# Held loads and moved state tiles in a fused S5 and long-convolution kernel

## The chip, the cores and the metric

The kernel runs on one core of one Trainium2 chip, as one program. The metric is device time in microseconds (us) of one execution; lower is better. A profiled execution gives the trace from which the rows below are taken. The engines are named as the trace names them: PE is the matrix engine, PEld its weight loads, DVE the vector engine, ACT the scalar engine, POOL the engine that issues the accumulating DMAs, SP the engine that issues nearly all other DMAs.

## The reference, cut to what matters

Two sequence layers read the same input `x` of 2048 positions and 1024 channels, and a gate mixes them.

```python
g = sigmoid((x * gate_w).sum(-1, keepdims=True))

# a: a diagonal complex state-space layer (S5)
Lam_bar = exp(dt * Lam)
Bu = einsum("bld,pd->blp", x, ((Lam_bar - 1.0) / Lam)[:, None] * Bmat)
for t in range(L):
    h = Lam_bar[None, :] * h + Bu[:, t, :]
    hs.append(h)
a = 2.0 * einsum("blp,dp->bld", stack(hs), Cmat).real + x * Dskip

# b: a short convolution of k, times v, then a long convolution by FFT
kv = (4-tap causal convolution of k with shift_k) * v
y = irfft(rfft(kv, 4096) * rfft(ssm_k, 4096))[:2048]
b = x * (y + kv * ssm_D)

out = g * a + (1 - g) * b
```

All inputs and the output are bfloat16.

## The kernel before, in words

The kernel first computes the long convolution (the "convolution stage", up to about 222 us), and then the state layer, the gate and the mix (the "state stage").

The convolution works on 8 chunks of 128 channels. For a chunk `n`, PE does the taps of the short convolution (`taps`, from the transposed `kT`), mirrors and transforms the filter (`mirror_K` from `kn`, then `fwd_K`) and the product kv (`times_v`, then `fwd_V`) with cosine and sine tables; ACT copies each transform from PSUM (`Kh`, which is kept in a part of BT 3 for even chunks, and `Vh`). DVE multiplies the two spectra in blocks (`products`, into `G`, with the scratch `wkh` and BT 2). PE then transforms back (`inverse`), ACT copies the result to `cv`, and SP stores it to a scratch in DRAM (`cv_scr`).

Some additions are not done by DVE but by DMAs that accumulate in SBUF. `gather` (line 125) issues them from POOL's queue: `G += wkh` in `products` (768 KB per chunk), `ks += lo` in `times_v`, `eok += lo` in `mirror_K`, and `hr += hr` in `turn_table`. DVE waits for the first of them in the middle of `products` (`G[:, :, 2:] += n1`).

The loads go through SP's queue, which issues in order. Those named `kn`, `kT`, `BT` and `xT` are transposing DMAs of 512 KB each (`load_t`, line 119; `xT` is one such load for each half of a block of 512 positions); `v` is a plain copy of 1 MB for two chunks, and `cv_scr` are plain stores. `load` (line 172) makes `kn`, `kT` and `v` of a chunk, `load_BT` (line 211) one half of a group of the state layer's B, `load_xT` (line 214) the transposed x of a block.

The order of the work is written out by hand. Helpers (`mm`, `tt`, `act` and so on, over `put` at line 91) fix the order on each engine as the order in which the program issues. The generators (`products`, `times_v`, `mirror_K`, `inverse`, `Bu_tile`, `turn_table`) yield between steps, and the loop at line 901 steps through them. In its pass `c`, called chunk c here, DVE does the products of chunk c, PE the inverse of chunk c - 1, the transforms of chunk c + 1, and the taps and mirror of chunk c + 2, and SP issues the loads of chunk c + 3.

Into this loop tiles of the state layer's first matmul are woven (`Bu_tile`: 32 matmuls of 128x256 with BT and xT, two copies of U by ACT, and a few matmuls with `lamd`, which `lam_diag` prepares on DVE). There are 12 of them, from the generator at line 899. Line 955 places one ahead of `fwd_K` in chunks 3 to 6, line 975 one ahead of `fwd_V` in chunks 2 and 4 and two in chunk 6; four are left for the time behind the loop. Chunk 1 and chunk 0 have none. Four tiles each use xT 0, xT 1 and xT 2, in this order; those that use xT 2 are the four behind the loop.

Of the kernel before, what the change touches and what calls it, by code (L numbers as in the profile page):

```python
# [10 lines left out]
ACT = mybir.ActivationFunctionType  # L11
# [9 lines left out]
def kernel(  # L21
# [40 lines left out]
    HB = TB // 2  # L62
    NG = NP // 2
    NC = D // 128
# [3 lines left out]
    def pool(name, bufs, **kw):  # L68
        return ctx.enter_context(tc.tile_pool(name=name, bufs=bufs, **kw))
# [6 lines left out]
    lam_pool = pool("lam", 1)  # L76
# [8 lines left out]
    def ps2(shape, name):  # L85
        return psum.tile(shape, F32, name=name, tag="ps")
# [4 lines left out]
    def put(eng, f, *a, **kw):  # L91
        with tc.issue_after(prev[eng]) if eng in prev else nullcontext():
            i = f(*a, **kw)  # L93
        prev[eng] = getattr(i, "ins", i)

    def mm(o, l, r, first, last):
        put("pe", nc.tensor.matmul, o, lhsT=l, rhs=r, start=first, stop=last)
# [9 lines left out]
    def ts(o, a, s1, s2, op0, op1=None):  # L107
        if op1 is None:
            put("dve", V.tensor_scalar, out=o, in0=a, scalar1=s1, scalar2=None, op0=op0)
        else:  # L110
            put("dve", V.tensor_scalar, out=o, in0=a, scalar1=s1, scalar2=s2, op0=op0, op1=op1)
# [4 lines left out]
    def act(o, i, **kw):  # L116
        put("act", nc.scalar.activation, out=o, in_=i, **kw)

    def load_t(o, i):
        put("sp", nc.sync.dma_start_transpose, out=o, in_=i)  # L120

    def move(o, i):
        put("sp", nc.sync.dma_start, out=o, in_=i)
# [37 lines left out]
    pih = consts.tile([128, 1], F32, name="pih")  # L161
# [7 lines left out]

    lds = {}  # L170

    def load(which, c):
        cc = slice(c * 128, (c + 1) * 128)
        if which == "kn":

            t = ld.tile([128, NT, 128], BF16, name="kn", tag="ld")
            load_t(t, B_ssm_k[cc, :])
        elif which == "v":

            w = 1 if c < 2 else 2  # L180
            if w == 1:
                t = ld.tile([128, NT, 1, 128], BF16, name="v", tag="ld")
            else:
                t = xt_pool.tile([128, NT, 2, 128], BF16, name="v2", tag="xT")
            move(t.rearrange("p n k d -> p n (k d)"),
                 vf.rearrange("(n p) d -> p n d", p=128)[:, :, c * 128:(c + w) * 128])
            for k in range(w):
                lds["v", c + k] = t[:, :, k]
            return
        else:  # L190

            t = ld.tile([128, PAD + S], BF16, name="kT", tag="ld")
            put("pool", nc.gpsimd.memset, t[:, 0:PAD], 0.0)
            load_t(t[:, PAD:], kf[:, cc])
        lds[which, c] = t
# [13 lines left out]
    xTs = {}  # L209

    def load_BT(g, c):
        load_t(BT[g][:, c], (A_B_re, A_B_im)[c][g * 256:(g + 1) * 256, :])

    def load_xT(tb, halves=(0, 1)):
        if 0 in halves:
            xTs[tb] = (xt_pool if tb in (1, 2) else xt_first).tile([128, ND, TB], BF16, name="xT", tag="xT")
        for h in halves:
            load_t(xTs[tb][:, :, h * HB:(h + 1) * HB], xf[tb * TB + h:(tb + 1) * TB:2, :])


# [297 lines left out]
    def spectrum(which, c):  # L518
        if which == "K" and c % 2 == 0:

            t = BT[3].rearrange("p c d q -> p (c d q)")
        elif which == "G":
            t = whole[c] = g_pool.tile([128, 4096], BF16, name="G")
        else:
            t = kv_pool.tile([128, 4096], BF16, name=which + "h", tag="kvh")
        k = 2 if c == 0 else 1
        return [t[:, h * 4096 // k:(h + 1) * 4096 // k].rearrange("p (c b f d) -> p c b f d", c=2, b=4, d=128)
                for h in range(k)]

    def of_tile(sp_, fi):  # L530
        nf = 4 // len(sp_)
        return sp_[fi // nf][:, :, :, fi % nf]

    def fwd_K(c, fis=range(NFI)):
        eo = eos["k", c]
        if c not in KH:
            KH[c] = spectrum("K", c)
        for fi in fis:
            fsl = slice(fi * 128, (fi + 1) * 128)
            ps = ps2([128, 2, 4, 128], "psk")  # L540
            for cc in range(2):
                tab = CF if cc == 0 else SF
                for mt in range(2):
                    mm(ps[:, cc], tab[:, mt, fsl], eo[:, cc, mt], mt == 0, False)
                for mt in range(2):
                    tb2 = (SF, NCF)[cc][:, mt, fsl]
                    mm(ps[:, cc, 1:4], tb2, eo[:, 1 - cc, mt, 0:3], False, mt == 1)
            act(of_tile(KH[c], fi), ps, func=ACT.Copy)

    def fwd_V(c, fis=range(NFI)):  # L550
        eo = eos["v", c]
        if c not in VH:
            VH[c] = spectrum("V", c)
        for fi in fis:
            fsl = slice(fi * 128, (fi + 1) * 128)
            ps = ps2([128, 2, 4, 128], "psv")
            for cc in range(2):
                tab = CF if cc == 0 else SF
                for mt in range(2):
                    mm(ps[:, cc], tab[:, mt, fsl], eo[cc][:, mt], mt == 0, mt == 1)  # L560
            act(of_tile(VH[c], fi), ps, func=ACT.Copy, scale=2.0 / 1024.0)
# [103 lines left out]
    def lam_diag(g, home, on_act=False):  # L665

        t = lamd[g] = home.tile([128, 2, 3, 128], BF16, name=f"lamd{g}")
        for j in range(2):
            for k, f in enumerate((lam[:, 0], lam[:, 1], mlam)):
                pi = 2 * g + j  # L670
                if on_act:
                    act(t[:, j, k], ident, func=ACT.Identity, scale=f[:, pi:pi + 1])
                else:
                    ts(t[:, j, k], ident, f[:, pi:pi + 1], None, ALU.mult)
# [170 lines left out]
    def step(gen):  # L845
        next(gen, None)
# [9 lines left out]
    none = iter(())  # L856
# [42 lines left out]
    tiles = (b for i in range(6) for b in Bu(i))  # L899

    for c in range(NC - 1):
        n, nn = c + 1, c + 2
        if c == 0:
            load("kn", 2)
            load("kT", 2)
            load("v", 2)
            load_BT(0, 0)
        if c == 0:
            p1 = products(0, 1)
            fwd_K(n, (0, 1))  # L910
            step(p0)
            run(tv)
            dg = dgs(nn, True)
            steps(p1, 2)
            step(p0)
            step(p1)
            run(p0)
            taps(nn, dg)
            step(sp)
            fwd_K(n, (2, 3))  # L920
            step(p1)
            run(sp)
            fwd_V(n)
            run(p1)
            run(fold_K(nn))
            tv = times_v(nn)
            step(tv)
            load("kn", 3)
            load("kT", 3)
            load("v", 4)  # L930
            load_BT(0, 1)
            continue
        tabs, back, prod = turn_table(c - 1) if c <= NG else none, inverse(c - 1), products(c)
        step(old)
        step(tabs)
        step(back)
        step(tv)
        steps(prod, 3)
        run(tv)
        step(old)  # L940
        step(tabs)
        run(back)
        run(old)
        if c == 1:
            load_xT(0)
        elif c == 2:
            load("v", 6)
            load_BT(1, 0)
        elif c == 3:
            load_BT(1, 1)  # L950
        elif c in (4, 6):
            load_xT(c // 2 - 1)
        if nn < NC:
            dg = dgs(nn)
        bu = next(tiles) if c >= 3 else none
        step(bu)
        fwd_K(n, (0, 1))
        step(bu)
        fwd_K(n, (2, 3))
        step(prod)  # L960
        fk = none
        if nn < NC:
            fk = mirror_K(nn)
            step(fk)
            taps(nn, dg)
        step(prod)
        run(fk)
        run(prod)
        if nn < NC:
            tv = times_v(nn)  # L970
            step(tv)
            if nn + 1 < NC:
                load("kn", nn + 1)
                load("kT", nn + 1)
        bu = [next(tiles) for _ in range({2: 1, 4: 1, 6: 2}.get(c, 0))] + [none, none]
        step(bu[0])
        fwd_V(n, (0, 1))
        step(bu[0])
        step(bu[1])
        fwd_V(n, (2, 3))  # L980
        step(bu[1])
        if c < 3:
            lam_diag(c - 1, lam_pool)
        old = tabs

    h3r.close()
    c = NC - 1
# [149 lines left out]
    tb = NTB - 1  # L1137
    t0 = tb * 4
    pss = []
    for tl in range(4):  # L1140
        ps = ps2([128, 2, 512], "psy")
        halves = [(slice(h * 512, h * 512 + 512), ps[:, h]) for h in range(2)]
# [41 lines left out]
```

## Time and profile before

| what | us |
|---|---|
| the three runs | 434.73, 427.0, 425.14 |
| their median | 427.0 |
| the profiled execution | 424.4 |
| its span in the trace | 422.6 |
| PE busy | 395.3 |
| DVE busy | 385.7 |
| ACT busy | 249.1 |
| POOL busy | 50.3 |

A row of the timeline gives the start in us from the span's start, the duration, the engine, the line (93, the helper, for nearly all), the operation, the tiles as out<-in, and how many it merges; behind it, in brackets, stands the idle time of the engine ahead of it and what ended that. Rows of SPq and of POOL DMAs are the time that the issuing takes; the transfer itself ends later ("to landing"). The stretches give, for each window, its length and the busy time of each engine.

### The profile page before, as it was taken

The page shows a single profiled execution, that of the slowest core. Times are in us where ns is not written, and L with a number is a line of the kernel's source. Part 1 is how long each engine was busy: PE and PEld are TensorE (multiplying, and loading weights), DVE is VectorE, ACT ScalarE, POOL GpSimd, SP SyncE. Part 2 cuts the span into 40 slices and gives each one's busy share as a digit, 9 for nine tenths or more (in the row PEclk, how much of TensorE's full clock was granted, in tenths as well). Part 3 has the DMA queues.
Part 4 walks back from the last instruction along what each step waited for, and adds up shares of the span by engine and source line. Part 5 has one row for each costly group of instructions (what it writes and reads, how often), then busy time and mean ns, then how long its engine had stood idle before and what let it go on. Part 6 is the DMA issues. An engine that isn't in the chain of part 4 may idle for free.

```text
span 422.6 us, 7462 instructions
## 1 busy us (share of the span) xinstructions
PE 395.3 (94%) x2957; PEld 253.6 (60%) x2985; DVE 385.7 (91%) x635; ACT 249.1 (59%) x332; POOL 50.3 (12%) x71
## 2 busy tenths in 40 slices
PE   7999796999979899898989999999999999899995
PEld 5556262566646566565877888874476674344442
DVE  8799999999999699988999999399999968799995
ACT  5897687868896668455437685733544243566101
POOL 3011030202112010100000000001220011232100
PEclk9999898999999999999999999999999999999999
DMA  7789899699979992395996990113873543999602
GB/s 151 150 186 211 191 185 200 137 173 171 205 163 158 94 223 52 64 113 76 208 182 182 171 206 2 27 25 80 195 163 74 113 111 90 214 216 213 129 1 100
DMA packets 126005, 59.23 MB, mean 140 GB/s; under 512 B 105993, under 2 KB 112913, under 8 KB 125970
## 3 DMA queue, kind: packets, MB, share of 16 engines
q1 hardware_dynamic: 117664, 42.22, 52.8%
q0 software_dynamic: 8224, 16.52, 23.7%
q8 instruction: 23, 0.38, 0.4%
q14 instruction: 12, 0.10, 0.1%
q10 hardware_dynamic: 82, 0.02, 0.0%
HBM read 12.86 MB, written 8.39 MB: 50 GB/s over the span
## 4 chain that ended last, share of the span: by engine, by line
DVE 35%; issue 34%; PE 16%; DMA 11%; POOL 2%; ACT 2%; DVEq 0%; POOLq 0%; SPq 0%
DMA G<-wkh 8%; DVE BT L93 7%; PE psy L93 6%; DVE wkh L93 6%; DVE G L93 6%; DVE t L93 4%; PE psk L93 3%; DVE W L93 2%; DMA pbb<-cv_scr 2%; PE psz L93 2%; DVE hb L93 1%; DVE A L93 1%; PE taps L93 1%; DVE q L93 1%; DVE trn L93 1%
## 5 line engine op out<-in xcount | busy, mean ns | idle before, releaser
L93 PEld LDWEIGHTS <-BT 128*128 128x128 bf16 x1024 | 100.0, 98 | 13.4
L93 PE MATMUL even<-xT,BT 128*128 128x256 bf16 x512 | 61.1, 273 | 0.0
L93 PE MATMUL odd<-xT,BT 128*128 128x256 bf16 x512 | 61.1, 272 | 0.0
L93 PE MATMUL psy<-CT,hb 128*128 128x512 bf16 x249 | 56.8, 379 | 1.6 <-DVE hb L93 1.3
L93 PE MATMUL psy<-CT,U 128*128 128x512 bf16 x251 | 56.3, 379 | 0.3
L93 PEld LDWEIGHTS <-hb 128*128 128x128 bf16 x256 | 24.8, 98 | 30.4 <-DVE hb L93 2.0
L93 PEld LDWEIGHTS <-U 128*128 128x128 bf16 x256 | 25.0, 98 | 29.8
L93 PE MATMUL psz<-G,CI 128*128 128x512 bf16 x64 | 26.1, 408 | 16.2 <-DVE G L93 16.2
L93 ACT ACTIVATE U<-even 128x512 bf16<-128x512 f32 x32 | 19.1, 596 | 34.0 <-PE even L93 34.0
L93 ACT ACTIVATE Vh<-psv 128x1024 bf16<-128x1024 f32 x32 | 30.7, 1037 | 8.5 <-PE psv L93 6.8
L93 DVE TENSOR_TENSOR_SCAN W<-rv,init,A 128x256 bf16<-128x256 f32 x48 | 32.2, 734 | 0.0
L93 PEld LDWEIGHTS <-SF 128*128 128x128 bf16 x192 | 18.8, 98 | 20.9 <-issue 2.0
L93 PE MATMUL taps<-dg,kT 128*128 128x128 bf16 x512 | 30.9, 221 | 0.3 <-DMA kT<-in_B_k_dram 0.3
L93 PEld LDWEIGHTS <-kT 128*128 128x128 bf16 x512 | 29.4, 99 | 1.5 <-DMA kT<-in_B_k_dram 0.8
L93 PE MATMUL psk<-eok,SF 128*128 128x512 bf16 (+1 forms) x128 | 29.4, 352 | 0.4
L93 ACT ACTIVATE U<-odd 128x512 bf16<-128x512 f32 x32 | 18.9, 594 | 15.8 <-PE odd L93 14.7
L93 ACT ACTIVATE cv<-psz 128x1024 bf16<-128x1024 f32 x16 | 16.5, 1028 | 16.5 <-PE psz L93 13.8
L93 PE MATMUL psz<-G,SI 128*128 128x512 bf16 x64 | 25.9, 404 | 0.0
L93 POOL DMA_DIRECT2D pbb<-gd x12 | 10.3, 860 | 123.4 <-ACT gd L93 122.2
L93 DVE TENSOR_TENSOR U<-U,q 128x512 bf16<-128x512 bf16 (+2 forms) x51 | 23.5, 489 | 0.6
L93 ACT ACTIVATE ga<-psy,gcols 128x1024 bf16<-128x1024 f32 x8 | 8.9, 1115 | 24.0 <-PE psy L93 24.0
L93 PEld LDWEIGHTS <-CI 128*128 128x128 bf16 x64 | 6.6, 103 | 26.6 <-DVE G L93 19.1
(164 smaller groups left out, 752.3 us busy)
## 6 DMA issues: line engine op xcount, KB each, us to landing
G<-wkh POOLq DMA_DIRECT2D x6, 768.0 KB, 8.2
cv_scr<-cv SPq DMA_DIRECT2D x16, 256.0 KB, 3.8
v<-in_B_v_dram SPq DMA_DIRECT2D x3, 1024.0 KB
pbb<-cv_scr SPq DMA_DIRECT2D x12, 256.0 KB, 5.0
xr<-in_A_x_dram SPq DMA_DIRECT2D x12, 256.0 KB, 4.7
pbb<-gd POOLq DMA_DIRECT2D x12, 256.0 KB, 3.4
ga<-xr POOLq DMA_DIRECT2D x8, 256.0 KB, 3.3
out_dram<-ga SPq DMA_DIRECT2D x8, 256.0 KB, 3.2
```

The costliest lines, as they stand in the source:

```text
L93: i = f(*a, **kw)
```

## The change

Three things are edited.

Loads of the convolution are held: in chunks 1 to 4, the load of `kn` is issued behind a write of one column of its tile by ACT, which stands behind the first two copies of `Vh`. SP issues in order, so `kT` and what else follows is held with it. The two halves of xT 2 are held by such writes as well.

x and B are loaded in other chunks: BT 0's second half and xT 0 at the end of chunk 0 (v of chunks 4 and 5 behind them), BT 1's halves behind kT in chunks 1 and 2, xT 1's halves behind kT in chunks 3 and 4, and xT 2 in chunk 6 behind `fwd_K`.

The state tiles go to `fwd_V` in chunks 1, 2, 3 and 5 and to `fwd_K` in chunk 4, one in each; chunk 6 keeps three. `lam_diag` moves to one chunk earlier.

```diff
+    def hold(column):
+        act(column, pih, func=ACT.Copy)
+
-    def load(which, c):
+    def load(which, c, held=False):
...
             t = ld.tile([128, NT, 128], BF16, name="kn", tag="ld")
+            if held:
+                hold(t[:, 0, 0:1])
             load_t(t, B_ssm_k[cc, :])
...
-    def load_xT(tb, halves=(0, 1)):
+    def load_xT(tb, halves=(0, 1), held=False):
...
         for h in halves:
+            if held:
+                hold(xTs[tb][:, 0, h * HB:h * HB + 1])
             load_t(xTs[tb][:, :, h * HB:(h + 1) * HB], xf[tb * TB + h:(tb + 1) * TB:2, :])
...
             load("kn", 3)
             load("kT", 3)
+            load_BT(0, 1)
+            load_xT(0)
+            lam_diag(0, lam_pool)
+            continue
+        if c == 1:
             load("v", 4)
-            load_BT(0, 1)
-            continue
...
-        if c == 1:
-            load_xT(0)
-        elif c == 2:
+        if c == 2:
             load("v", 6)
-            load_BT(1, 0)
-        elif c == 3:
-            load_BT(1, 1)
-        elif c in (4, 6):
-            load_xT(c // 2 - 1)
...
-        bu = next(tiles) if c >= 3 else none
+        bu = next(tiles) if c in (4, 6) else none
         step(bu)
         fwd_K(n, (0, 1))
         step(bu)
         fwd_K(n, (2, 3))
+        if c == 6:
+            load_xT(2, held=True)
...
-            if nn + 1 < NC:
-                load("kn", nn + 1)
-                load("kT", nn + 1)
-        bu = [next(tiles) for _ in range({2: 1, 4: 1, 6: 2}.get(c, 0))] + [none, none]
+        bu = [next(tiles) for _ in range({1: 1, 2: 1, 3: 1, 5: 1, 6: 2}.get(c, 0))] + [none, none]
         step(bu[0])
         fwd_V(n, (0, 1))
+        if nn + 1 < NC:
+            load("kn", nn + 1, True)
+            load("kT", nn + 1)
+        if c in (1, 2):
+            load_BT(1, c - 1)
+        elif c in (3, 4):
+            load_xT(1, (c - 3,))
         step(bu[0])
         step(bu[1])
         fwd_V(n, (2, 3))
         step(bu[1])
-        if c < 3:
-            lam_diag(c - 1, lam_pool)
+        if c == 1:
+            lam_diag(1, lam_pool)
```

## The prediction

> **What bounds the kernel now.** I read the stretches first, cut at the first product of each chunk of the convolution (chunk 1 starts at 48.30, chunk 6 at 171.76). Columns: length, then busy time of each engine.
>
> ```profile
> core 0: us, PE busy (x) PEld busy (x) DVE busy (x) ACT busy (x) POOL busy (x), PEclk, DMA share, GB/s
> 48.30:72.77 24.47, 20.04 (x135) 10.77 (x135) 24.40 (x28) 18.84 (x26) 3.95 (x5) 0.92 0.95 171
> 72.77:97.23 24.46, 23.18 (x173) 14.25 (x174) 24.39 (x28) 18.57 (x25) 3.95 (x5) 0.98 1.01 157
> 97.23:120.72 23.49, 20.68 (x164) 13.27 (x165) 23.42 (x21) 20.43 (x32) 3.95 (x5) 1.00 1.14 200
> 120.72:148.27 27.55, 25.59 (x205) 17.20 (x205) 23.43 (x21) 20.08 (x30) 3.95 (x5) 1.00 1.03 125
> 148.27:171.76 23.49, 21.76 (x173) 13.78 (x173) 23.42 (x22) 17.09 (x22) 2.96 (x3) 1.00 0.63 122
> 171.76:198.07 26.31, 24.50 (x180) 16.77 (x180) 22.46 (x20) 14.62 (x19) 1.20 (x1) 1.00 0.84 91
> ```
>
> DVE fills chunks 1, 2, 3 and 5 to the last tenth. Only chunks 4 and 6 hold time in which DVE stands: 4.12 and 3.85 us. The waits of DVE between 40 and 222 us, and its timeline, say on what:
>
> ```profile
> DVE G L93 <- DMA G<-wkh: 7.8, 2, 4.1
> ...
> 140.72 1.23 DVE L93 TENSOR_TENSOR G<-G,wkh 128x2048 bf16<-128x2048 bf16 x1 [4.09 <-DMA G<-wkh]
> ...
> 192.14 1.22 DVE L93 TENSOR_TENSOR G<-G,wkh 128x2048 bf16<-128x2048 bf16 x1 [3.75 <-DMA G<-wkh]
> ```
>
> Both are the accumulating transfer of 768 KB into G. POOL's timeline has its issue, and the transfer groups of the stretches round chunks 3, 4, 5 and 6 (in that order) its time to landing:
>
> ```profile
> 101.48 1.20 POOL L93 DMA_DIRECT2D G<-wkh  x1 [14.55 <-DVE wkh L93]
> ...
> 124.97 1.20 POOL L93 DMA_DIRECT2D G<-wkh  x1 [9.75 <-DVE wkh L93]
> ...
> 152.52 1.20 POOL L93 DMA_DIRECT2D G<-wkh  x1 [9.75 <-DVE wkh L93]
> ...
> 176.01 1.20 POOL L93 DMA_DIRECT2D G<-wkh  x1 [10.52 <-DVE wkh L93]
> ...
> G<-wkh POOLq DMA_DIRECT2D x1, 768.0 KB, 8.1
> ...
> G<-wkh POOLq DMA_DIRECT2D x1, 768.0 KB, 15.7
> ...
> G<-wkh POOLq DMA_DIRECT2D x1, 768.0 KB, 6.6
> ...
> G<-wkh POOLq DMA_DIRECT2D x1, 768.0 KB, 16.0
> ```
>
> The issue comes 4.25 us after the chunk's start (124.97 - 120.72; chunks 3, 5 and 6 alike), and DVE has 140.72 - 4.09 - 124.97 = 11.66 us of other work. 6.6 and 8.1 fit in that; 15.7 and 16.0 don't. What differs is on SP's queue:
>
> ```profile
> 42.50 5.42 SPq L93 DMA_TRANSPOSE BT<-in_A_B_im_dram  x1
> ...
> 54.17 11.48 SPq L93 DMA_TRANSPOSE xT<-in_A_x_dram  x2
> ...
> 104.78 5.95 SPq L93 DMA_TRANSPOSE BT<-in_A_B_im_dram  x1
> ...
> 117.64 2.11 SPq L93 DMA_TRANSPOSE kT<-in_B_k_dram  x1
> 122.72 2.48 SPq L93 DMA_DIRECT2D cv_scr<-cv  x2
> 125.29 17.48 SPq L93 DMA_TRANSPOSE xT<-in_A_x_dram  x2
> 142.87 5.92 SPq L93 DMA_TRANSPOSE kn<-in_B_ssm_k_dram  x1
> 148.97 2.47 SPq L93 DMA_TRANSPOSE kT<-in_B_k_dram  x1
> ...
> 176.41 15.75 SPq L93 DMA_TRANSPOSE xT<-in_A_x_dram  x2
> ```
>
> In chunks 4 and 6 two halves of x go out 0.32 and 0.40 us behind the gather and run beside all of it. In chunk 5 the last transposing load (148.97 + 2.47) ends 1.08 us ahead of the gather: 6.6 us. In chunk 3 the next one follows by 3.30 us: 8.1 us.
>
> **The change, part by part.** *Holds.* Four kn loads (chunks 1 to 4, kT behind each on SP) and the two halves of xT 2 wait for a one-column write on ACT. The trace has no such write; the nearest is the four-column `ends` copy:
>
> ```profile
> 64.68 3.77 ACT L93 ACTIVATE Vh<-psv 128x1024 bf16<-128x1024 f32 x4 [0.60 <-PE psv L93]
> ...
> 103.01 0.21 ACT L93 ACTIVATE ends<-U 128x4 bf16<-128x4 bf16 x1
> ...
> 114.53 3.77 ACT L93 ACTIVATE Vh<-psv 128x1024 bf16<-128x1024 f32 x4
> ...
> 142.80 1.94 ACT L93 ACTIVATE Vh<-psv 128x1024 bf16<-128x1024 f32 x2 [2.14 <-PE psv L93]
> ...
> 145.10 1.96 ACT L93 ACTIVATE Vh<-psv 128x1024 bf16<-128x1024 f32 x2
> ...
> 195.06 1.94 ACT L93 ACTIVATE Vh<-psv 128x1024 bf16<-128x1024 f32 x2 [1.77 <-remote]
> ```
>
> Six at 0.21 are 1.3 us on ACT, which is busy 14.6 to 20.4 us of a chunk: hidden, 0 on the path (without that cover 1.3). Each also waits for the old user of its buffer, done a chunk ago. Behind a held kn stand kT, one load of B or x, and the next chunk's cv stores; ACT's cv copy waits for stores a whole chunk old, so nobody is late by that.
>
> *Do the held loads fit before the next gather?* The hold opens behind the second Vh copy. Chunk 3: 114.53 + 1.9 + 0.2 = 116.6, next gather 124.97: 8.4 us. Chunk 4: 142.80 + 1.94 less the state tile that leaves (3.83, below) is 140.9, with the hold 141.1; next gather 152.52 - 4.09 = 148.43: 7.3 us. Chunk 1, with its new tile ahead: 64.68 + 1.9 + 3.4 - 0.8 + 0.2 = 69.4, next gather 72.77 + 0.97 + 4.25 = 77.99: 8.6 us. To be issued are three transposes of 512 KB. One costs SP 2.11 or 2.47 us where no gather runs (kT), 5.92 where one does (kn). As the gathers are over when the hold opens I take 2.3 each, 6.9 in all: it fits, by 0.4 us in chunk 4 and 1.5 or more elsewhere. Ends: 6.3 (three at 2.11) and 17.8 (three at 5.92), which would not fit. Chunk 3's 3.30 us of grace shows that an overrun of about 1 us is harmless.
>
> *xT 0 and v.* xT 0 goes out behind B's load (42.50), in chunk 0, with no gather near: from about 44.5, two at 2.3, done by 49 to 50, against a gather at 48.30 + 0.97 + 4.25 = 53.5 (other end: 11.48, done at 59.4 and across it). The v load moves behind it: 0, it is used a chunk later.
>
> *Chunk 4* loses the x loads beside its gather: its wait of 4.09 goes. What is late next is PE:
>
> ```profile
> 64.05 0.59 PE L93 MATMUL psv<-ks,SF 128*128 128x512 bf16 x2 [0.82 <-DMA ks<-lo]
> ...
> 70.80 0.61 PE L93 MATMUL psz<-G,CI 128*128 128x512 bf16 x1 [3.56 <-DVE G L93]
> ...
> 170.77 0.39 PE L93 MATMUL psz<-G,CI 128*128 128x512 bf16 x1 [1.63 <-DVE G L93]
> ...
> 195.29 0.59 PE L93 MATMUL psv<-ks,SF 128*128 128x512 bf16 x2
> ...
> 198.22 0.39 PE L93 MATMUL psz<-G,CI 128*128 128x512 bf16 x1 [1.79 <-DVE G L93]
> ```
>
> Chunk 5's product needs the last Vh, at 145.10 + 1.96 = 147.06, while DVE would be there at 148.27 - 4.09 = 144.18. With both tiles left in chunk 4, 2.88 of the 4.09 would be given back. But the change takes one tile away: 25.59 - 21.76 = 3.83 us of PE, so Vh comes at 143.2, 0.95 ahead of DVE. The whole 4.09 counts.
>
> *Chunk 1* gets that tile. PE stood 0.82 + 3.56 = 4.38 there, so 3.83 fits: 0 (uncovered, 3.83). Chunks 3 and 5 move theirs from the K to the V transform: same sum, 0. *lamd* moves a chunk earlier: chunks 1 and 2 are 0.97 longer than chunk 3 for it; chunk 0 gains 0.97, chunk 2 loses it: 0.
>
> *Chunk 6* keeps three tiles. The gather has its queue to itself and lands in 6.6 to 8.1; xT 2 goes out ahead of ACT's V copies and first serves in chunk 7. The wait of 3.75 goes, but PE has no gap from 170.77 to 195.88 (of the 26.31 us of the chunk it is busy 24.50, and the rest is the 1.79 ahead of 198.22), and the last Vh ends at 195.06 + 1.94 = 197.00. DVE, free at 198.07 - 3.75 = 194.32, then waits for Vh: only 198.07 - 197.00 = 1.07 is kept. Chunk 7 and the state stage after 222 carry no edit and shift whole.
>
> Sum: 4.09 + 1.07 = 5.16. The profiled execution took 424.4 (span 422.6): 419.2. It lies 2.6 below the median of the three runs, 427.0; the mean of the two lower runs, 425.14 and 427.0, is 426.1, and 426.1 - 5.16 = 420.9, rounded to **421.0**, is what I forecast for a timed run.
>
> **The rivals.** *(a) The held loads overrun (slower).* If a transpose costs nearer 5.92 than 2.3, the three are still going out when the gather of chunks 2, 3, 4 and 5 is issued. For it: only 0.4 us of room in chunk 4, and SP's 17.48 and 15.75 for two. Against it: 2.11 and 2.47 where no gather ran. It decides from about 2.43 us a load in chunk 4 and 2.8 in chunk 3 (8.4 / 3), about 1 us later with the grace. Each such gather would cost 4.09: 4 x 4.09 = 16.4 on top of 421.0 is 437; two chunks, 429.
>
> *(b) The gathers aren't slowed by the loads (no change).* Between 120 and 148 us the two queues had:
>
> ```profile
> q1 hardware_dynamic: 6124, 2.00, 72.4%
> q0 software_dynamic: 680, 1.55, 30.8%
> ```
>
> That is 0.308 x 16 x 28 / 680 = 0.203 us a gather packet and 0.053 a load packet. If each of the 16 engines took one of each in turn, a gather of 8.1 would grow by 0.053 / 0.203 = 26%, to 10.2: under 11.66, no wait at all. The loads could then not be the cause, and 426.1 would stay. The Trainium skill (DMA: Bandwidth & Descriptors, "Queues, rings and completion order") says so: an engine goes round-robin over its queue rows, packet by packet. By that rule the hold is worth nothing; the 15.7 and 16.0 beside loads of x, against 6.6 without, don't agree with it. For (b) otherwise: chunk 3's gather shared its time with B's load from 104.78.
>
> *(c) Chunk 6 gives all of its wait:* 7.84 in all, 418.3. For it only that PE's records have modelled ends; against it the gapless PE from 170.77.
>
> *(d) A part of it:* one chunk collides (chunk 4's 7.3 us, or xT 0 in chunk 1), 421.0 + 4.09 = 425.1.
>
> **How the numbers follow.** Forecast 0.60 (its own range 419 to 423), (a) 0.13, (b) 0.06, (c) 0.09, (d) 0.12. Range 417 to 429: it leaves out most of (a) and a little below (c). Two per cent, 8.5 us, is about what a measurement of this kernel can tell from no change (its three runs span 425.14 to 434.73). Faster by that, below 418.5: half of (c) and a tenth of the forecast, 0.11. Slower, above 435.5: (a) with all four chunks, three quarters of it, 0.10. The rest 0.79.
>
> **What would show it.** Right: every G gather at 5.8 to 9 us to landing, no DVE wait on it in chunks 4 and 6, a new DVE wait of about 2.7 us on Vh at chunk 7's first product, chunk 4 at 23.5 us, chunk 1 with PE idle under 1 us, and three transposes issued in about 7 us behind each hold. Wrong: DVE waits for G in chunks 2 to 5, SP transposes of 5 us behind a hold, ACT standing before a hold, or chunk 4's next product waiting for Vh.

## The result and the profile after

The changed kernel takes **419.9 us** (median of four runs, 419.81 to 420.83), the kernel before 427.09 on the same chip (425.14 to 434.73). The ratio is 0.985, with a 95% interval of 0.982 to 0.988: a gain that is there, and under two per cent. The forecast was 421.0, with 0.79 of the chances on a change of less than two per cent. In some executions the granted clock is lower and the time some per cent longer; the ratios leave these out, and where such an execution is the profiled one its clock is given.

The profiled execution took 419.92 (span 418.1) against 424.4, so 4.48 us less; the forecast sum was 5.16. The stretches of the kernel after, cut as before at the first product of each chunk (1 to 7; columns as in the prediction):

```profile
core 0: us, PE busy (x) PEld busy (x) DVE busy (x) ACT busy (x) POOL busy (x), PEclk, DMA share, GB/s
49.78:74.24 24.46, 21.66 (x166) 13.56 (x167) 24.39 (x27) 19.96 (x29) 3.95 (x5) 0.98 0.92 182
74.24:97.72 23.48, 22.37 (x166) 13.78 (x167) 23.41 (x21) 17.62 (x25) 3.95 (x5) 0.95 0.84 182
97.72:121.21 23.49, 21.66 (x169) 13.66 (x169) 23.42 (x22) 20.28 (x31) 3.95 (x5) 1.00 0.79 155
121.21:144.69 23.48, 21.66 (x169) 13.66 (x169) 23.41 (x21) 19.93 (x31) 3.95 (x5) 1.00 0.83 163
144.69:168.17 23.48, 21.75 (x173) 13.75 (x173) 23.41 (x21) 16.98 (x22) 2.95 (x3) 1.00 0.69 129
168.17:193.44 25.27, 25.11 (x184) 17.18 (x185) 22.55 (x20) 14.33 (x21) 1.20 (x1) 1.00 0.55 103
193.44:216.39 22.95, 22.50 (x262) 18.35 (x259) 22.84 (x18) 8.91 (x19) 0.00 (x0) 0.93 1.08 198
```

Compare the lengths with those of before. Chunk 4 went from 27.55 to 23.48 (4.07 less), chunk 6 from 26.31 to 25.27 (1.04 less), chunk 2 from 24.46 to 23.48 (0.98 less, the lamd work). The others stayed within 0.01. Chunk 1 begins 1.48 later (49.78 against 48.30). Together 4.07 + 1.04 + 0.98 - 1.48 = 4.61, and chunk 7 begins 198.07 - 193.44 = 4.63 earlier: nothing else in the loop moved.

The waits of DVE between 40 and 222 us are now a single row, and the timeline says where it is:

```profile
DVE G L93 <- ACT Vh L93: 2.6, 1, 2.6
```

```profile
193.44 2.29 DVE L93 TENSOR_TENSOR G<-Kh,Vh 128x4096 bf16<-128x4096 bf16 x1 [2.58 <-ACT Vh L93]
```

The two waits for the transfer into G (4.09 and 3.75) are gone. In their place stands one wait for Vh, at the first product of chunk 7. The transfer groups give the six gathers of 768 KB at their median time to landing. The view of the tile G counts two transfers of 384 KB ahead of chunk 1 as well, so of its three numbers the last, the slowest, is the one to read:

```profile
G<-wkh POOLq DMA_DIRECT2D x6, 768.0 KB, 7.8
```

```profile
DMA to landing us min/median/max: 5.9/7.6/8.3
```

The slowest of them, 8.3, is far below the 11.66 us of other work that DVE has. The timeline shows how the hold does it. Its rows here, in order of time, are ACT's write in chunk 3, SP's issues behind it, POOL's next gather, and the same for chunk 4:

```profile
117.32 0.21 ACT L93 ACTIVATE kn<-pih 128x1 bf16<-128x1 f32 x1
117.55 2.10 SPq L93 DMA_TRANSPOSE kn<-in_B_ssm_k_dram  x1
119.82 2.48 SPq L93 DMA_TRANSPOSE kT<-in_B_k_dram  x1
122.39 2.81 SPq L93 DMA_TRANSPOSE xT<-in_A_x_dram  x1
125.29 1.00 SPq L93 DMA_DIRECT2D cv_scr<-cv  x2
125.45 1.20 POOL L93 DMA_DIRECT2D G<-wkh  x1 [14.13 <-DVE wkh L93]
...
141.29 0.22 ACT L93 ACTIVATE kn<-pih 128x1 bf16<-128x1 f32 x1
141.53 2.09 SPq L93 DMA_TRANSPOSE kn<-in_B_ssm_k_dram  x1
143.79 2.19 SPq L93 DMA_TRANSPOSE kT<-in_B_k_dram  x1
146.03 2.24 SPq L93 DMA_TRANSPOSE xT<-in_A_x_dram  x1
148.32 24.37 SPq L93 DMA_DIRECT2D cv_scr<-cv  x4
148.94 1.20 POOL L93 DMA_DIRECT2D G<-wkh  x1 [9.74 <-DVE wkh L93]
```

SP starts 0.02 us after the one-column write ends, issues three transposing loads at 2.1 to 2.8 each, and is through 0.25 us (125.20 to 125.45) and 0.67 us (148.27 to 148.94) before the gather is issued.

### The profile page after: what moved, and what is told of

It reads as the page before. It is cut to its first block, busy times and chain, and to the rows that moved or that the text cites. A ratio compares the mean times of both kernels' runs of the same rounds, so it can differ in the third digit from the quotient of the medians.

```text
span 418.1 us, 7475 instructions
## 1 busy us (share of the span) xinstructions
PE 396.8 (95%) x2957; PEld 254.6 (61%) x2985; DVE 385.7 (92%) x635; ACT 249.0 (60%) x338; POOL 50.2 (12%) x71
## 4 chain that ended last, share of the span: by engine, by line
DVE 38%; issue 30%; PE 23%; DMA 4%; ACT 2%; POOL 1%; another core or an unknown queue 0%; DVEq 0%; POOLq 0%; SPq 0%
PE psy L93 12%; DVE BT L93 10%; DVE wkh L93 9%; DVE G L93 5%; DVE t L93 5%; PE psk L93 3%; PE psz L93 2%; PE odd L93 2%; DMA pbb<-cv_scr 2%; DVE ks L93 2%; PE taps L93 1%; PE psv L93 1%; DVE W L93 1%; PE even L93 1%; DMA ga<-xr 1%
## 5 line engine op out<-in xcount | busy, mean ns | idle before, releaser
L93 PE MATMUL even<-xT,BT 128*128 128x256 bf16 x512 | 62.1, 275 | 0.0
L93 PE MATMUL psz<-G,CI 128*128 128x512 bf16 x64 | 25.1, 392 | 11.9 <-DVE G L93 11.8
L93 PE MATMUL taps<-dg,kT 128*128 128x128 bf16 x512 | 31.8, 225 | 0.1
L93 PEld LDWEIGHTS <-kT 128*128 128x128 bf16 x512 | 30.3, 101 | 1.3 <-DMA kT<-in_B_k_dram 0.6
L93 PE MATMUL psk<-eok,SF 128*128 128x384 bf16 (+1 forms) x126 | 29.0, 352 | 0.3
L93 POOL DMA_DIRECT2D pbb<-gd x12 | 10.3, 859 | 124.7 <-ACT gd L93 123.5
L93 PE MATMUL psz<-G,SI 128*128 128x512 bf16 x64 | 25.0, 391 | 0.0
L93 POOL DMA_DIRECT2D G<-wkh x8 | 9.7, 1218 | 106.3 <-DVE wkh L93 106.3
```

## The experiments

The theory on trial: transposing loads issued just behind a gather stretch it, the hold puts them ahead of it, and the moved tile lets chunk 4 keep the whole wait. The rivals are those of the prediction. Each kernel is told by its edit against the kernel it starts from; each ratio is against the kernel before, timed on the same chip.

### Only the loads of x held: x_held

From the kernel before; tiles, kn, kT and B stay where they were.

```diff
-        elif c in (4, 6):
-            load_xT(c // 2 - 1)
...
         fwd_K(n, (2, 3))
+        if c in (4, 6):
+            load_xT(c // 2 - 1, held=True)
```

> The kernel before with one edit: the loads of xT 1 and xT 2 in chunks 4 and 6 stand behind fwd_K and behind a one-column write on ACT. No other load and no state tile is moved, so chunk 4 keeps two tiles. Load theory (the x loads beside the gather stretch it, and PE is what is late next): both G gathers land in 6 to 9 us, DVE waits for neither; chunk 5's first product then waits 2.5 to 3 us for Vh, because PE still has two tiles in chunk 4, and chunk 7's first product 2.6 us for Vh. Chunk 4 is 26.4 us long, chunk 6 25.3; the profiled time is 424.4 - 1.2 - 1.1 = 422.1. Rival (the moved tile does nothing, the x loads are all of it): chunk 4 is 23.5 us and the time 419.5. Rival (the loads are not the cause): gathers stay at 15.7 and 16.0, time 424.4.

Measured: 427.64 (423.66 to 429.48 in nine runs, a tenth at 431.36), ratio 1.000 (0.996 to 1.005). The profiled execution was the one of 431.36, at a mean granted clock of 0.971. Its DVE waits and the gathers' times to landing:

```profile
DVE G L93 <- ACT Vh L93: 8.6, 3, 4.3
```

```profile
DMA to landing us min/median/max: 6.0/6.8/8.2
```

No gather is slow any more and none is waited for, and yet the time did not move: DVE now waits 8.6 us for Vh, where it waited 7.8 for G. Of the 8.6, 2.44 stand behind chunk 3, which has no edit and where the granted clock was 0.87, and 4.27 behind chunk 6, at 0.94; how much of these belongs to the clock can't be read from this execution. The other 1.94 stand behind chunk 4, at full clock, in which PE had no gap (columns as above):

```profile
127.03:152.55 25.52, 25.52 (x206) 17.28 (x205) 23.51 (x20) 21.23 (x34) 3.95 (x5) 1.00 0.83 153
```

So PE is what is late next in chunk 4. The expected time of 422.1 was missed: no run is under 423.66, and the interval allows a gain of 0.4%, 1.7 us, at most, where 2.3 were expected. What took the rest is not shown. What the run does show is that freeing the gather alone is not what the change earns.

### The same bytes without the transposition: x_plain

From the kernel before. The loads of xT 1 and xT 2 become plain copies of the same bytes into the same tiles at the same place, so those two blocks of x are left untransposed.

```diff
-            load_t(xTs[tb][:, :, h * HB:(h + 1) * HB], xf[tb * TB + h:(tb + 1) * TB:2, :])
+            if tb in (1, 2):
+                r0 = tb * TB + h * HB
+                move(xTs[tb][:, :, h * HB:(h + 1) * HB],
+                     xf[r0:r0 + HB, :].rearrange("(p a) (d t) -> p (a d) t", a=2, t=HB))
+            else:
+                load_t(xTs[tb][:, :, h * HB:(h + 1) * HB], xf[tb * TB + h:(tb + 1) * TB:2, :])
```

> The kernel before with xT 1 and xT 2 loaded by plain copies of the same number of bytes from the same rows, issued at the same place beside the gathers of chunks 4 and 6 (the blocks are then not transposed, so the state layer and the gate of these two blocks get other values). Theory A (it is the transposing that stretches the gather): both gathers land in 6 to 9 us, no DVE wait on G, time 422.1 as in x_held. Theory B (any load of this size beside it does, by its share of bytes or packets): gathers stay at 12 to 16 us, DVE waits 1 to 4 us for each, time 423 to 424.5.

Measured: 424.21 (423.6 to 432.04, ten runs), ratio 0.996 (0.992 to 1.0005); profiled 423.65. Its timeline of DVE between 120 and 205 us has these two waits, and its gathers land so:

```profile
146.90 2.29 DVE L93 TENSOR_TENSOR G<-Kh,Vh 128x4096 bf16<-128x4096 bf16 x1 [2.43 <-ACT Vh L93]
...
195.67 2.29 DVE L93 TENSOR_TENSOR G<-Kh,Vh 128x4096 bf16<-128x4096 bf16 x1 [2.58 <-ACT Vh L93]
```

```profile
DMA to landing us min/median/max: 6.3/7.6/11.4
```

The clean pair is chunk 6: the copies go out 0.39 us behind the gather (175.04 against 174.65), as close as before (0.40), and it takes 11.4 instead of 16.0, which is under the 12.38 us (192.14 - 3.75 - 176.01) that DVE has there. (In chunk 4 they came 1.40 behind, and it took 8.4.) So traffic issued right behind a gather does stretch it, and the transposition stretches it more than the bytes do, past what DVE has to cover it. The 11.4 lies between the two theories (6 to 9, and 12 to 16), so neither held whole. And with both tiles left in chunk 4, the freed 4.09 comes back as a 2.43 wait for Vh: the prediction had said 2.88. Chunk 7 begins at 195.67 against 198.07, 2.4 earlier. Of this the profiled time keeps 0.75 (423.65 against 424.4). From 218.62 to 235.67, behind the loop, the granted clock was 0.90, and PE did 128 matmuls in 17.05 us where before did 143 at 1.00.

### The change without the holds: no_hold

From the kernel after: only ACT's writes are taken out; loads and tiles keep their places in the program.

```diff
     def hold(column):
-        act(column, pih, func=ACT.Copy)
+        pass
```

> The changed kernel with the one-column writes of ACT taken out: loads in the new chunks, tiles in the new places, but kn and xT 2 go out as soon as SP gets to them. Load theory: kn goes out beside the gathers of chunks 1, 3 and 4 and behind the v copy in chunk 2, xT 2 beside the gather of chunk 6. That gather lands in about 16 us and DVE waits 3.75 for it in place of the 2.58 for Vh (1.2 more); gathers beside one kn land in 10 to 13 us and cost 0 to 2 us each: 421 to 426. Rival (the new order of the loads is what counts, the holds do nothing): 419.9, gathers at 7 to 8.5.

Measured: 424.14 (422.36 to 432.88, ten runs), ratio 0.9925 (0.988 to 0.997); profiled 427.01. DVE's waits for a DMA in the timeline, and the six gathers by chunk, 1 to 6:

```profile
92.81 1.23 DVE L93 TENSOR_TENSOR G<-G,wkh 128x2048 bf16<-128x2048 bf16 x1 [2.98 <-DMA G<-wkh]
142.09 1.23 DVE L93 TENSOR_TENSOR G<-G,wkh 128x2048 bf16<-128x2048 bf16 x1 [1.02 <-DMA G<-wkh]
194.39 1.23 DVE L93 TENSOR_TENSOR G<-G,wkh 128x2048 bf16<-128x2048 bf16 x1 [4.63 <-DMA G<-wkh]
```

```profile
G<-wkh POOLq DMA_DIRECT2D x1, 768.0 KB, 9.0
G<-wkh POOLq DMA_DIRECT2D x1, 768.0 KB, 14.5
G<-wkh POOLq DMA_DIRECT2D x1, 768.0 KB, 7.0
G<-wkh POOLq DMA_DIRECT2D x1, 768.0 KB, 12.6
G<-wkh POOLq DMA_DIRECT2D x1, 768.0 KB, 7.1
G<-wkh POOLq DMA_DIRECT2D x1, 768.0 KB, 16.9
```

Without the hold SP runs ahead, and its transposing loads fall behind the gathers again. The gathers of chunks 2, 4 and 6 are issued at 78.17, 129.41 and 177.38, and SP's timeline has right behind them

```profile
79.03 15.14 SPq L93 DMA_TRANSPOSE kn<-in_B_ssm_k_dram  x1
...
129.81 3.67 SPq L93 DMA_TRANSPOSE kn<-in_B_ssm_k_dram  x1
...
177.78 16.43 SPq L93 DMA_TRANSPOSE xT<-in_A_x_dram  x2
```

0.86 (there the copy of v goes out first, at 0.42), 0.40 and 0.40 us later. In chunks 1 and 3 the next load follows by 1.04 and 2.13, and the gathers take 9.0 and 7.0. The waits for G sum to 8.63, with 1.23 for Vh; after has 2.58 for Vh alone. The difference, 8.63 + 1.23 - 2.58 = 7.28, is close to what the two profiled executions differ by (427.01 - 419.92 = 7.09). The lowest runs differ by less (422.36 against 419.81: 2.55). Whether SP ran into fewer gathers in those is not shown, as only one execution was profiled. By the ratios, about half of the gain is left without the holds: 0.9925, where the kernel after has 0.985 here and 0.988 in a second measurement below, whose interval (0.982 to 0.994) overlaps that of no_hold.

### The change with the tiles in their old places: tiles_back

From the kernel after.

```diff
-        bu = next(tiles) if c in (4, 6) else none
+        bu = next(tiles) if c >= 3 else none
...
-        bu = [next(tiles) for _ in range({1: 1, 2: 1, 3: 1, 5: 1, 6: 2}.get(c, 0))] + [none, none]
+        bu = [next(tiles) for _ in range({2: 1, 4: 1, 6: 2}.get(c, 0))] + [none, none]
```

> The changed kernel with the state tiles where they were before (none in chunk 1, two in chunk 4), loads and holds as changed. Theory (PE is next in chunk 4): in the changed kernel chunk 4's last Vh ends 1.36 us ahead of DVE (143.33 against 144.69); a tile of 3.83 us more makes it 2.5 us late, so chunk 4 is about 26.0 us, with a DVE wait of 2.5 on Vh, and the time 422.4. Rival (the tiles don't matter, PE has room): 419.9, chunk 4 at 23.5.

Measured: 427.18 (426.61 to 432.34, ten runs), ratio 1.0035 (0.999 to 1.008): the whole gain is lost. DVE's two long waits in the timeline round chunk 5, and SP's load and PE's row that explain the second:

```profile
146.96 2.29 DVE L93 TENSOR_TENSOR G<-Kh,Vh 128x4096 bf16<-128x4096 bf16 x1 [2.51 <-ACT Vh L93]
169.24 0.69 DVE L93 TENSOR_TENSOR eok<-kn,lo 128x1024 bf16<-128x1024 bf16 x1 [5.10 <-ACT lo L93]
```

```profile
150.13 1.97 SPq L93 DMA_TRANSPOSE xT<-in_A_x_dram  x1
...
155.27 3.59 PE L93 MATMUL odd<-xT,BT 128*128 128x256 bf16 x16 [5.80 <-DMA xT<-in_A_x_dram]
```

The first wait is the expected one: two tiles in chunk 4 hold Vh back, 2.51. The second was in nobody's expectation. A tile ahead of `fwd_K` in chunk 5 needs the second half of xT 1, which the change issues only behind the hold of chunk 4, here at 150.13, when chunk 5 has begun and 1.09 us ahead of its gather. PE stands 5.80 us for that load with all that follows, and DVE is 5.10 late. Chunk 7 begins at 201.04 against 193.44, 7.60 later; the two waits are 7.61, and the smaller differences (chunk 1 begins 0.59 earlier, for one) about cancel. The rows show what PE waited for; no run moved that tile alone.

### The hold 2 us later, and the hold earlier: late_hold, late_last, early_hold

All from the kernel after. late_hold issues the held loads behind both halves of `fwd_V` (the rest of that block moves with them), to let them overrun the gather's issue; early_hold issues them ahead of `fwd_V`, while other accumulating transfers (`ks`, `eok`, `hr`) still run. late_last is late_hold run a second time. The edit of late_hold:

```diff
+        step(bu[0])
+        step(bu[1])
+        fwd_V(n, (2, 3))
+        step(bu[1])
         if nn + 1 < NC:
             load("kn", nn + 1, True)
...
-        step(bu[0])
-        step(bu[1])
-        fwd_V(n, (2, 3))
-        step(bu[1])
```

And early_hold:

```diff
-        fwd_V(n, (0, 1))
         if nn + 1 < NC:
             load("kn", nn + 1, True)
...
+        fwd_V(n, (0, 1))
         step(bu[0])
```

> The changed kernel with the held loads of chunks 1 to 4 put behind the whole of fwd_V, so that each hold opens behind the fourth copy of Vh, about 2 to 2.5 us later. In the changed kernel the last of the three transposing loads ends its issue 2.66, 0.88, 0.25 and 0.67 us ahead of the gather of chunks 2, 3, 4 and 5; here it ends about 1.4 to 2.2 us behind the gather's issue in chunks 3, 4 and 5. Overrun theory (rival a of the prediction): those gathers land in 10 to 16 us, DVE waits 0 to 4 us for each of two or three of them, time 421 to 430. Grace theory (a transposing load that was queued ahead of the gather and overlaps only its start is harmless): gathers at 8 to 10 us, inside the 11.66 that DVE has, time 419.9.

Measured, late_hold: 419.41 (419.33 to 420.16, four runs), ratio 0.982 (0.979 to 0.985), no worse than the change. SP's last held load in chunks 3 and 4 goes out at

```profile
124.83 1.96 SPq L93 DMA_TRANSPOSE xT<-in_A_x_dram  x1
...
148.43 2.00 SPq L93 DMA_TRANSPOSE xT<-in_A_x_dram  x1
```

and the gathers of chunks 4 and 5 are issued at 125.15 and 148.64, so 0.32 and 0.21 us behind the start of a load that is still being issued for 1.6 to 1.8 us more. G's view:

```profile
DMA to landing us min/median/max: 6.0/8.9/9.6
```

The two gathers themselves land in 9.1 and 8.6 us, 1.7 and 0.7 longer than in the kernel after (7.4 and 7.9), not twice as long. So an overrun of 1.6 to 1.8 us by a load that began ahead of the gather costs nothing, and rival (a) falls as far as that. A held load that *begins* behind the gather was not made here; no_hold has such loads, and they cost.

> The kernel with the holds behind the whole of fwd_V once more, for one more look at its gathers: landing at 8.5 to 9.6 us for chunks 1 to 5, no DVE wait on G (grace theory). Overrun theory: a gather at 12 us or more in one of them.

Measured, late_last: 424.87 in its one run, against 419.41. Its gathers (up to 11.9, in chunk 2, where the copy of v came 0.52 us behind; more on this below) are waited for 0.3 us only, and most of what differs lies elsewhere. DVE waits 3.53 us for PE at 16.37, in the opening, ahead of the loop, and chunk 1 begins at 52.31 (49.45 in late_hold), the last inverse at 219.32 (216.24), so of the 5.46 us 2.86 was lost ahead of the loop, 0.22 in it, and the rest behind it. It tells little on the hold, but shows what a single run is worth.

> The changed kernel with the holds of chunks 1 to 4 ahead of the first copy of Vh in place of behind the second, so that they open 2 to 4 us earlier. The transposing loads then run beside the end of the accumulating transfers into ks, hr and eok. Theory (only the gather into G has a reader that comes soon enough to wait, 11.66 us behind its issue): eok's landing grows from 4 to 8 us to 8 to 14, DVE and PE wait for none of it or PE under 1 us, time 419.9. Rival (the small transfers matter as well, as the name of the change says): PE or DVE waits for ks, hr or eok of 1 to 4 us a chunk, time 422 to 430.

Measured, early_hold: 420.67 (419.98 to 421.21, four runs), ratio 0.984 (0.980 to 0.988). No G wait; of the other accumulating transfers, `ks` grows to 10.3 at most (9.3 in the kernel after) and `eok`, expected at 8 to 14, to 8.5 (7.6), and all it costs is one row in PE's waits:

```profile
PE psv L93 <- DMA ks<-lo: 1.0, 1, 1.0
```

So the place of the hold makes no difference that can be told here, from ahead of `fwd_V` to behind it. It must only keep the transposing loads from going out right behind a gather into G.

### Taking the new wait away: two_in_5, last_in_6, both_5_6, after_again

The kernel after is left with DVE's 2.58 for Vh at chunk 7, since three tiles stand ahead of the last `fwd_V`. last_in_6 keeps chunk 6's three and puts the last of them behind the second half of `fwd_V`:

```diff
         step(bu[0])
-        step(bu[1])
         fwd_V(n, (2, 3))
         step(bu[1])
+        step(bu[1])
```

two_in_5 has this and takes one of chunk 6's tiles to chunk 5, where it is the one behind `fwd_V`:

```diff
-        bu = [next(tiles) for _ in range({1: 1, 2: 1, 3: 1, 5: 1, 6: 2}.get(c, 0))] + [none, none]
+        bu = [next(tiles) for _ in range({1: 1, 2: 1, 3: 1, 5: 2, 6: 1}.get(c, 0))] + [none, none]
```

both_5_6 is two_in_5 with the tile that is left to chunk 6's `fwd_V` begun between its halves and ended behind them:

```diff
-        step(bu[0])
+        if c < 6:
+            step(bu[0])
         fwd_V(n, (0, 1))
...
         step(bu[0])
         fwd_V(n, (2, 3))
-        step(bu[1])
-        step(bu[1])
+        run(bu[0])
+        run(bu[1])
```

> The changed kernel with one of chunk 6's three state tiles moved behind fwd_V of chunk 5, where PE stands 1.7 us; chunk 6 keeps two. Theory (PE is the bound from chunk 6 to the end of the convolution): the 1.7 us and the 0.6 that PE still stands ahead of the last inverse are used, the 2.58 us of DVE's wait on Vh shrinks to under 0.8, and the time falls by about 2 to 417.6. Rival (DVE's wait is worth all of itself): 417.3. Rival (PE late at chunk 6's start delays its K transform and nothing is won): 419.9.

> The changed kernel with chunk 6's last state tile put behind the second half of fwd_V in place of ahead of it. The sum of PE's work up to the last inverse is the same, so if PE is the bound there, DVE's wait of 2.58 on Vh goes but comes back as a longer wait of PE-bound work: PE stood only 0.6 us ahead of the last inverse, so the time falls by no more than about 0.6, to 419.3. Rival (DVE's wait is the loss): all of 2.58 is kept, 417.3.

Measured: two_in_5 420.01 (419.0 to 420.53, four runs), ratio 0.983 (0.980 to 0.986); last_in_6 **418.4** (417.66 to 419.4, four runs), ratio 0.980 (0.976 to 0.983). Chunk 7's first product in DVE's timeline, first two_in_5, then last_in_6:

```profile
192.25 2.29 DVE L93 TENSOR_TENSOR G<-Kh,Vh 128x4096 bf16<-128x4096 bf16 x1 [1.38 <-ACT Vh L93]
```

```profile
190.86 2.28 DVE L93 TENSOR_TENSOR G<-Kh,Vh 128x4096 bf16<-128x4096 bf16 x1
```

two_in_5 missed its expectation of 417.6: 1.38 of the wait is left where under 0.8 was expected, and its median is that of the kernel after. In last_in_6 the wait is gone, and chunk 7 begins 2.58 earlier than in the kernel after; the profiled time is 419.92 - 417.66 = 2.26 less. I had expected at most 0.6, from the 0.59 us that PE stands ahead of the last inverse in the kernel after. That was a misreading, and late_hold's profile shows why. PE's row at that place in after and in late_hold:

```profile
216.54 0.39 PE L93 MATMUL psz<-G,CI 128*128 128x512 bf16 x1 [0.59 <-DVE G L93]
```

```profile
216.24 0.39 PE L93 MATMUL psz<-G,CI 128*128 128x512 bf16 x1 [2.26 <-DVE G L93]
```

In after's profiled execution the granted clock dipped in chunk 7 (0.93 in the last stretch above), PE was busy 22.50 us there where late_hold has 20.83 at 1.00 (as many matmuls, 262), and this filled most of its gap; DVE set the end all the same. The second profile of the kernel after (after_again) has 0.59 once more, at 0.93 once more. In last_in_6 PE has no wait left there: its last inverse starts at 214.20, 2.34 earlier, so PE takes 0.24 of the 2.58.

> The changed kernel with one of chunk 6's state tiles behind fwd_V of chunk 5, and chunk 6's other one behind its own fwd_V. With only the last tile moved behind fwd_V, DVE's wait of 2.58 went and PE had no wait left ahead of the last inverse, so PE was just late there; this one also uses the 1.63 that PE stands in chunk 5. Theory (PE and DVE then meet within 1 us): DVE waits for neither Vh nor G from chunk 1 on, chunk 7's first product starts 2.6 earlier than in the changed kernel, time 417.3 to 418.0. Rival (the second tile in chunk 5 makes chunk 6's K transform and Vh late, as the 1.38 us wait in the run with two tiles in chunk 5 alone): 419.

> The changed kernel unedited, as the base for the other two of this call: 419.9, DVE wait of 2.6 us on Vh at chunk 7's first product, no wait on G.

Measured, on one chip: both_5_6 **417.82** (417.35 to 419.77, six runs), ratio 0.981 (0.976 to 0.986); the kernel after 420.62 (419.34 to 423.61, six runs), ratio 0.988 (0.982 to 0.994), and its profile repeats the first: 2.59 of wait for Vh at chunk 7, none for G. The intervals overlap, so the 2.8 us between them is a difference of medians and no more. In both_5_6's profiled execution (418.95) the waits of DVE are

```profile
DVE G L93 <- DMA G<-wkh: 0.9, 1, 0.9
DVE G L93 <- ACT Vh L93: 0.8, 1, 0.8
```

The 0.9 is in chunk 2. Its gather there and SP's next rows, and the same two in the kernel after:

```profile
78.22 1.20 POOL L93 DMA_DIRECT2D G<-wkh  x1 [14.39 <-DVE wkh L93]
...
78.80 0.40 SPq L93 DMA_DIRECT2D v<-in_B_v_dram  x1
```

```profile
78.49 1.20 POOL L93 DMA_DIRECT2D G<-wkh  x1 [16.08 <-DVE wkh L93]
...
79.51 0.39 SPq L93 DMA_DIRECT2D v<-in_B_v_dram  x1
```

The plain copy of v, 1 MB and not held, follows the gather by 0.58 us in both_5_6, and the gather takes 12.5; by 1.02 us in the kernel after, and it takes 8.0. In two_in_5, last_in_6 and late_last it followed by 0.52 and the gather took 11.8 to 11.9. So a load need not transpose to hurt a little. Holding v as well was not tried.

With last_in_6 (on another chip) it is the fastest kernel of this study; both beat the kernel before by about 2%.

## Why the prediction was right, point by point

**What bounds the kernel, and the cause of the two waits.** Right. The gathers fell from 15.7 and 16.0 to 7.4 and 7.0, and no_hold brings the stretching back by the order of the loads alone. x_plain narrows the cause: 1 MB of plain copies right behind a gather brings 11.4 to 12.5, at the edge of its cover, and the same transposing 15.7 to 16.9. One step was too wide: the prediction blamed loads that "run beside all of it". Before the change two halves of x went out 1.62 us behind chunk 1's gather and ran beside it, and it landed in 8.2; the first 0.6 us or so are what counts (see the last section). Rival (b) falls, and so does, here, its estimate by the turn-by-turn rule of the Trainium skill (DMA: Bandwidth & Descriptors, "Queues, rings and completion order"), with one packet of the profile to a turn: it gave 10.2 beside the loads, which is near the 11.4 beside the plain copies of x, but the runs show 12.6 to 16.9 with a transposing load issued 0.32 to 0.86 us behind the gather (and once, in chunk 2 of x_plain, 11.0).

**Chunk 4 keeps the whole 4.09.** Right: 4.07. That the moved tile is the condition is shown twice, by the 2.43 of x_plain and the 2.51 of tiles_back; the prediction had 2.88.

**Chunk 6 keeps 1.07 of 3.75.** Right: 1.04, with a wait of 2.58 for Vh where "about 2.7" was named. That PE, with three tiles, is what makes Vh late is shown by last_in_6, where one tile behind `fwd_V` removes the wait. Rival (c) falls.

**The held loads fit.** Right in outcome, for a reason that was too narrow. Three of them took 7.65 and 6.74 us from the hold on (6.9 predicted), with 0.25 and 0.67 us left (1.5 and 0.4 predicted). But late_hold shows that fitting is not the condition: the last load must begin ahead of the gather, and need not be through. So the threshold of rival (a), 2.43 us a load, was too strict; it counted a collision that a load *ahead* of the gather doesn't cause. The prediction's own ground for some grace, the 3.30 us by which a load *followed* chunk 3's gather, says nothing about an overrun.

**The hold costs nothing on ACT; xT 0 in chunk 0 costs nothing.** Right for the write: 0.20 to 0.22 each, and neither PE nor DVE waits for ACT because of it. xT 0 went out at 44.74 to 51.27, later than the 49 to 50 expected and 2.8 us before the next gather, which landed in 8.3.

**A tile in chunk 1.** Cost 0 as predicted (24.46 against 24.47), but the sign named for it was wrong: PE still stands 24.46 - 21.66 = 2.80 there, not under 1. The 4.38 of before was the idle time of a stretch with a granted clock of 0.92; after has 0.98. PE's 20.04 and the tile's 3.83 would be 23.87, and 21.66 were measured: if all of it went with the clock it would be 23.87 x 0.92 / 0.98 = 22.4 (an estimate), so the clock may be 1.5 of the 2.2, and the rest stays open.

**Chunks 3 and 5, "from the K to the V transform: same sum, 0".** This step failed as reasoning, though its number held. The sum of PE's work is the same, but the tile's place decides whether xT 1's second half is there yet. Kept ahead of `fwd_K` in chunk 5 with the loads moved, it costs 5.10. The prediction asked only what covers an edit, and not what another edit of the same change had taken from under it. The move is a needed part, not a neutral one.

**lamd.** 0.98 gained in chunk 2, 1.48 paid in chunk 0. The 0.51 more than lamd's 0.97 was lost ahead of every edited instruction: the first product of the opening (G<-BT,Vh) that DVE waits for stands at 19.77 in the kernel before and at 20.29 here. In the second profile of the changed kernel it stands at 19.84, and chunk 1 at 49.35, 1.05 later than before, so this part varies between executions. It is the main part of the distance between 5.16 and 4.48.

**From the profile to the median.** The forecast added the distance of the profiled execution to the two lower runs (421.0), and the measured median is 419.9. By medians the change is worth 7.2 us, by the lowest runs 5.3, by the two traces 4.5. So it is in part luck that 421.0 came within 1.1 of the median: the sum was 0.7 above what the traces give and 2.0 below what the medians give, and the base of 426.1 was 1.0 below the median of the kernel before. A part of the distance may go with the clock: the ten timed runs of the changed kernel (both chips) had granted clocks of 0.983 to 0.994, those of the kernel before on the three chips of the experiments 0.971 to 0.991. Whether the changed kernel is granted more, and why, is not settled here.

## What to carry to other kernels

Look up what is issued within about 0.6 us (the bound seen here) behind an accumulating DMA that an engine waits for: if it is a large load, a transposing one above all, hold it back, for which a one-column write into its tile, by an engine whose order already marks the moment, is enough. When a wait is freed, ask which engine is next at that place and move its work out of the way in the same change; here the freed gather alone earned nothing that could be measured. And when loads and the work that uses them are both moved, check each use against its load's new place before calling a move neutral.

## What the runs showed of the hardware

What mattered for a gather of 768 KB was what followed it on SP's queue in the first 0.6 us or so. First load behind its issue, and its time to landing: one transposing load of 512 KB after 0.40 us, 12.6; two of them after 0.32 to 0.40, 15.7 to 16.9; plain copies of 1 MB in all after 0.39 to 0.58, 11.4 to 12.5; such a copy after 0.42 with a transposing load behind it at 0.86, 14.5 (in chunk 2 of x_plain, after 0.07 and 0.51, only 11.0). Loads that came a little later did next to nothing: the copy of v after 0.87 with a transposing load at 1.31 (chunk 2 of before), 8.2; v alone after 1.02, 8.0; kn after 1.04 and 2.13, 9.0 and 7.0; two halves of x after 1.62 (chunk 1 of before), 8.2. Nor did small ones: plain stores of cv after 0.28 to 0.31 us left it at 8.0 (chunk 3 of tiles_back, chunk 4 of after_again). Transposing loads issued 0.14 to 0.36 us *ahead* of it (late_hold and late_last, chunks 4 and 5) let it land in 8.6 to 9.8. The load can suffer as well: from 3.67 to 15.14 us of SP's time for one transposing load behind a gather (no_hold), about 2 to 3 where none runs. Why the first half microsecond decides no run here shows.
